# Key-feature sums from a Gram product, and six more split products of w_out, in an attention and SwiGLU kernel

## The chip, the core and the metric

The kernel is one program for one core of a Trainium2 chip. The metric is the device time of one execution in microseconds (us); three runs of the kernel before gave 276.74, 276.76 and 276.82, so its time is the median, 276.76. All profile rows are from one profiled execution of that kernel.

Engines are named as the profile names them: PE (TensorE, matmuls), PEld (its weight loads), DVE (VectorE), ACT (ScalarE), POOL (GpSimd), SP (SyncE, which issues DMAs). Every engine works through its own queue in order.

## What is computed

Four batches of four heads, 1088 positions, 32 numbers each, go through a linear attention, and its output through a SwiGLU block.

```python
def phi(x):                                   # 64 features from two sketches of 8
    a = np.einsum('rd,bhsd->bhsr', S1, x)
    b = np.einsum('rd,bhsd->bhsr', S2, x)
    return np.einsum('bhsi,bhsj->bhsij', a, b).reshape(*x.shape[:-1], r * r)
q_p, k_p = phi(q), phi(k)
kv = np.einsum('bhsf,bhsd->bhfd', k_p, v)
z = np.sum(k_p, axis=2)                       # the feature sums
num = np.einsum('bhsf,bhfd->bhsd', q_p, kv)
den = np.einsum('bhsf,bhf->bhs', q_p, z)[..., None] + 1e-06
x = (num / den)  ->  (4352, 128)
g = x @ w_gate                                # 128 -> 1536
out = (g * sigmoid(g) * (x @ w_val)) @ w_out  # 1536 -> 128
```

`z` for features i, j of one head is the sum over positions of `a_i * b_j`, which is an entry of the 8 x 8 matrix product of `a` transposed and `b`.

## The kernel before, in words

Everything is written out by hand in one order; nothing is scheduled afterwards. The 4352 tokens are cut into ten blocks: three small ones of batch 1 (384, 320, 384 tokens), then six of 480 and a last one of 384. The 1536 hidden features are twelve chunks of 128. One block and one chunk make a **unit**: two products (gate and value) of the block's x with 128 columns of the weights, a Silu on ACT, a product on DVE (the hidden chunk, into a slot of `hbuf`), and later a **down** product of the hidden chunk with 128 rows of `w_out` into a PSUM bank that collects the block's output.

The units of the last seven blocks are the loop at L1405 and are numbered y = 0 to 83 here: block `line[m]`, chunk j is y = 12 m + j. Each step of that loop starts unit y + 1 (`start_unit`, L983), finishes unit y (`finish_unit`, L994) and does one down product, that of unit y - 5.

**Split products.** A float32 product costs two instructions of two passes each. For the weights and for x the kernel uses three float32r products instead: a number is cut into a high part, a low part and a difference, and the exact product is put together from `wd*xd`, `w1*x1` and `wb*x0`. In a unit these are the two products of L989, a scaling by ACT in place in PSUM (L992), then four products (L1001, L1002); then Silu (L1004, ACT) and the hidden product (L1009, DVE), which frees the unit's pair of PSUM banks. Three such pairs go round, so unit y + 3 starts in the pair of unit y.

The down product is either plain (L1077, float32) or split (L1069, L1071, L1072), as the list `DOWN` says (L888 to L890): 6 chunks of `line[2]`, 9 each of `line[3]` to `line[5]`, 7 of the last block. For a split one, `cut_hidden` (L951) cuts the hidden chunk three steps ahead: h1 by ACT (L968) or DVE (L966) at step y + 1, h0 by POOL (L969) at y + 2, hd by DVE (L972) at y + 3. The parts lie in six sets of three tiles, taken in turn, in buffers that were used for loading k, q, v and for early hidden chunks. `w_out` is cut by `cut_down` (L903) in steps y = 20 to 28, into a tile that takes the place of `room`. In a block with split products the plain ones use `scaled`, a copy of `w_out` times -1, because the block is put together by a subtraction (L1105).

**Attention of batches 2 to 4** runs beside the units, in a generator (`attentions`, L615) that is stepped once per unit, from y = 20 on once in two. For a batch: transposes of k on DVE (L327), key sketches on PE (L354), copied out by ACT (L590; L630 for batch 2, which copies one of the two sketches and leaves the other in PSUM), the 64 features per key on DVE (L377), their products with v (`key_values`, L388), and the feature sums: POOL adds nine pieces (L547), four products with ones add the partitions (L713), and `fold` (L597) multiplies by the first sketch matrix and adds over i with three DVE instructions, into a column block of `s123`. `query_sketches` (L342) then gives numerator sketches and denominator at once. `query_step` (L737) makes the query features on DVE (L741 to L748, then L377 and the transposes of L758 in three pieces), and `numerators` (L766) multiplies them (L776) and copies x out. `numerators` stands at y = 4, 20 and 40. x itself is cut by ACT (L865), POOL (L868) and DVE (L873).

Of the kernel before, what the change touches and what calls it, by code (L numbers as in the profile page):

```python
# [7 lines left out]
FP32 = mybir.dt.float32  # L8
# [11 lines left out]
def kernel(  # L20
# [129 lines left out]
    wg = const.tile([P, NCH, P], FP32, name="wg")  # L150
    wv = const.tile([P, NCH, P], FP32, name="wv")
# [159 lines left out]
    NL = 10  # L311
    hbuf = const.tile([P, NH - NL, BW], FP32, name="hbuf")
    late = const.tile([P, NL, BW], FP32, tag="late", name="late", bufs=1)
    slots = [(hbuf[:, k, :] if k < NH - NL else late[:, k - NH + NL, :]) for k in range(NH)]
# [8 lines left out]
    own2 = const.tile([P, 2 * H], FP32, name="own2")  # L323
# [219 lines left out]
    def feature_sums(phk):  # L543

        rows = phk[:].rearrange("p c h i j -> p c (h i j)")
        s = apool.tile([P, 4, H * F], FP32, tag="zs", name="zs")[:, 0:2, :]
        add = lambda o, a, b: nc.gpsimd.tensor_tensor(out=o, in0=a, in1=b, op=ALU.add)  # L547

        def last():
            add(s[:, 0, :], s[:, 0, :], s[:, 1, :])  # L550
            add(s[:, 0, :], s[:, 0, :], rows[:, 8, :])

        return s[:, 0, :], [
            lambda: add(s, rows[:, 0:2, :], rows[:, 2:4, :]),
            lambda: add(s, s, rows[:, 4:6, :]),
            lambda: add(s, s, rows[:, 6:8, :]),
            last,
        ]

    def beside(gen, steps):  # L560

        for x in gen:
            if steps:
                steps.pop(0)()
            yield x

# [30 lines left out]
    def fold(kv):  # L597

        t = apool.tile([P, R, R], FP32, tag="fold", name="fold")
        w = apool.tile([P, R], FP32, tag="w", name="w")  # L600
        nc.vector.tensor_tensor(
            out=t[:], in0=kv[:, F : 2 * F].rearrange("p (i j) -> p i j", j=R),
            in1=sq[:, 0, :, :], op=ALU.mult,
        )
        nc.vector.tensor_reduce(
            out=w[:], in_=t[:].rearrange("p i j -> p j i"), axis=AX.X, op=ALU.add
        )
        nc.vector.tensor_tensor(
            out=s123[:, :, 2, :],
            in0=w[:].unsqueeze(1).to_broadcast([P, 2 * H, R]),  # L610
            in1=own2[:].unsqueeze(2).to_broadcast([P, 2 * H, R]),
            op=ALU.mult,
        )

    def attentions():  # L615
# [5 lines left out]
        for i, c in enumerate(kpieces):  # L621
            key_products(kp[:, i, :], *c)
        ka = apool.tile([P, NC * H, R], FP32, tag="kas", name="kas")

        def sketch(ps, i):
            c0, c1 = kpieces[i]
            return ps[:, i, 0 : 64 * (c1 - c0)].rearrange("p (x t r) -> p x t r", t=2, r=R)

        for i, (c0, c1) in enumerate(kpieces):
            nc.scalar.copy(ka[:, H * c0 : H * c1, :], sketch(kp, i)[:, :, 0, :])  # L630
        yield from turn_queries(1)
        phk = apool.tile([P, NC, H, R, R], FP32, tag="phk", name="phk")
        for n, (i, c0, c1) in enumerate(((0, 0, 3), (0, 3, 5), (1, 5, 7), (1, 7, 9))):
            first = H * (c0 - kpieces[i][0])
            kb = sketch(kp, i)[:, first : first + H * (c1 - c0), 1, :]
            key_features(phk, (ka[:, H * c0 : H * c1, :], kb), c0, c1)
            if n == 0:
                zs, sums = feature_sums(phk)
            else:
                sums.pop(0)()  # L640
            if n == 3:
                let_go("keys")
            if n % 3 != 1:
                yield
        sums.pop(0)()
        yield from turn_keys(2)
        kvz = pair("values")
        key_values(kvz[:, 0, 0:F], phk, 0, NC)
        kab, copies = sketched(pair(), key_products, 2, "kab2")
        run_copies(copies, 2)  # L650
        value_sums(kvz[:, 0, :], zs)
        fold(kvz[:, 0, :])
# [12 lines left out]
        zs, sums = feature_sums(phk)  # L665
        for f in sums:
            f()
        yield from turn_keys(3)
        yield from turn_queries(2)
        for b in (2, 3):  # L670
            yield "pe"
            if b == 3:
                numerators(2, spread)
            kv = bank("g2")
            key_values(kv[:, 0:F], phk, 0, NC)
            if b == 2:
                kab, copies = sketched(pair(), key_products, 2, "kab2")
                run_copies(copies, 2)
            value_sums(kv, zs)
            fold(kv)  # L680
            spread = spread_out(b, kv)
            yield
            yield "pe"
            qab, copies = sketched(pair(), query_sketches, 3, "qab")
            run_copies(copies, 2)
            yield
            if b == 2:
                yield from turn_queries(3)
# [20 lines left out]

    def value_sums(kv, zs):  # L710

        for h in range(H):
            nc.tensor.matmul(  # L713
                kv[32 * h : 32 * h + 32, F : 2 * F], ones[:], zs[:, F * h : F * h + F],
                start=True, stop=True,
            )
# [186 lines left out]
    def cut_down():  # L903

        n = len(FINE)
        parts = const.tile([P, 3, n, D], F32R, tag="room", name="dparts", bufs=1)
        w1, wb, wd = (parts[:, k] for k in range(3))
        scaled = apool.tile([P, len(PLAIN), D], FP32, tag="zs", name="scaled")
        low = const.tile([P, n, D], FP32, tag="late", name="dlow", bufs=1)
        down_parts.update(w1=w1, wb=wb, wd=wd, scaled=scaled)  # L910
        rest = [(0, slice(0, 1)), (1, slice(1, 8, 2)), (5, slice(6, 7)), (6, slice(NCH - 1, NCH))]

        def high(c):
            nc.scalar.activation(w1[:, c], wo[:, FINE[0] :][:, c], AF.Copy, scale=CUT)

        def left(c):
            nc.gpsimd.tensor_tensor(
                out=low[:, c], in0=wo[:, FINE[0] :][:, c], in1=whole(w1[:, c]), op=ALU.subtract
            )

        def scale(c):
            nc.scalar.activation(wb[:, c], low[:, c], AF.Copy, scale=BETA)

        def differ(c):
            nc.gpsimd.tensor_tensor(
                out=wd[:, c], in0=whole(w1[:, c]), in1=whole(wb[:, c]), op=ALU.subtract
            )

        def other(k, c):
            m = len(range(NCH)[c])  # L930
            nc.scalar.activation(scaled[:, k : k + m, :], wo[:, c, :], AF.Copy, scale=-1.0)


        def exchange():
            for k, c in zip((1, 3, 4), (8, 9, 10)):
                PLAIN[k] = c
                nc.scalar.activation(scaled[:, k, :], wo[:, c, :], AF.Copy, scale=-1.0)

        add_to(behind, NCH * 5 + 8, exchange)

        a, b, c = slice(0, 3), slice(3, 6), slice(6, n)
        for step in (
            [(high, a)], [(left, a), (high, b)], [(left, b), (scale, a)], [(differ, a), (high, c)],
            [(left, c), (scale, b)], [(differ, b), (scale, c)], [(differ, c), (other, *rest[0])],
            [(other, *rest[1])], [(other, *rest[2]), (other, *rest[3])],
        ):
            for f, *args in step:
                f(*args)
            yield

    def cut_hidden(y, i, j):  # L951

        if not h_sets:
            x = []
            for tag in ("kld", "qld", "vld", "kT", "qT"):
                t = const.tile([P, 2, WB], F32R, tag=tag, name="h" + tag, bufs=1)
                x += [t[:, k, :] for k in range(2)]
            t = const.tile([P, 8, WB], F32R, tag="late", name="hlate", bufs=1)
            x += [t[:, k, :] for k in range(8)]
            h_sets.extend(x[k : k + 3] for k in range(0, 18, 3))  # L960
# [4 lines left out]
        if j in (2, 5, 8, 10) and i != line[2]:  # L965
# [11 lines left out]
    room = const.tile([P, 10, BW], FP32, tag="room", name="room", bufs=1)  # L977
# [39 lines left out]
    def unit(i, j, late=False, between=(None, None), apart=False):  # L1017
# [10 lines left out]
        sg = room[:, len(lates) + caught[0], :] if late else fpool.tile([P, WB], FP32, tag="sg", name="sg", bufs=5)  # L1028
# [25 lines left out]
    def down(y=None):  # L1054
# [11 lines left out]
        if j in mine:  # L1066
            w1, wb, wd = [down_parts[x][:, FINE.index(j), :] for x in ("w1", "wb", "wd")]
# [7 lines left out]
        else:  # L1075
            w = down_parts["scaled"][:, PLAIN.index(j), :] if mine else wo[:, j, :]
# [390 lines left out]
```

## Time and profile before

| What | Value |
|---|---|
| time, median of 3 runs | 276.76 us (276.74 to 276.82) |
| the profiled execution, span from first to last instruction | 275.1 us |
| PE, DVE, ACT, POOL busy | 268.8, 214.1, 193.6, 105.7 us |
| granted TensorE clock | 1.00 in every stretch, 0.97 in the last 9 us |

The profile gives no device time of the profiled execution apart from its span, so 1.66 us of the median lie around the span.

Busy time of the engines by stretch of the span (us):

| Stretch | what runs | PE | DVE | ACT | POOL |
|---|---|---|---|---|---|
| 48 to 70 | last units of the first blocks, keys of batch 2 | 22.00 of 22 | 20.28 | 10.46 | 12.30 |
| 70 to 108 | into the loop, batch 2 queries, keys of batch 3 | 38.00 of 38 | 27.59 | 25.76 | 12.06 |
| 108 to 143 | y = 8 to 21 | 35.00 of 35 | 24.77 | 22.59 | 7.28 |
| 143 to 183 | y = 21 to 39, `cut_down`, batch 4 queries | 39.92 of 40 | 28.86 | 34.35 | 17.55 |
| 183 to 266 | y = 40 to 83 | 83.00 of 83 | 71.86 | 70.78 | 40.77 |

How to read it. A busy PE is not a PE at its peak, since matmuls are pipelined. What one product costs the kernel is the time from its start to the start of the next one, which the chain of work that ended last gives, instruction by instruction. A row of a timeline has start, duration, engine, line, operation and shape; two rows of one engine may overlap a little, so that a product of 0.65 us on DVE takes 0.57 us of its queue. In brackets stands what idle time before it waited for.

### The profile page before, as it was taken

The numbers are of one execution on the slowest core, as the hardware profiler recorded it, in microseconds if no ns is written. First come the engines' busy times: TensorE is split into PE (matmuls) and PEld (weight loads), VectorE is DVE, ScalarE is ACT, GpSimd is POOL, SyncE is SP. The second block draws the span as 40 slices with busy tenths as digits, with TensorE's granted clock in tenths as the row PEclk, the third lists the DMA queues.
The fourth block names the chain that finished last, engine by engine and source line by source line (L and its number), as shares of the span: only waits on it lengthen the run. The fifth ranks groups of instructions, "written<-read, shape, count | busy, mean of one in ns | idle before, by whom it ended". The sixth has DMA issues, their size and how long they took to land.

```text
span 275.1 us, 5788 instructions
## 1 busy us (share of the span) xinstructions
PE 268.8 (98%) x2191; PEld 200.5 (73%) x2191; DVE 214.1 (78%) x373; ACT 193.6 (70%) x349; POOL 105.7 (38%) x117
## 2 busy tenths in 40 slices
PE   7999999999999999999999999999999999999995
PEld 6645566666785786777577777867887888789994
DVE  3997988989788773887545766967987995998871
ACT  2468666462685686677479898769879888897880
POOL 3313422149350640260034353435535663553330
PEclk9999999999999999999999999999999999999999
DMA  6573196122231043000200020000100200010021
GB/s 191 172 216 87 49 270 200 60 104 62 62 88 23 4 111 99 2 0 0 38 12 4 1 38 0 0 2 11 26 2 0 36 1 0 13 25 1 2 36 29
DMA packets 26139, 14.30 MB, mean 52 GB/s; under 512 B 19840, under 2 KB 24192, under 8 KB 26112
## 3 DMA queue, kind: packets, MB, share of 16 engines
q1 hardware_dynamic: 25456, 13.84, 19.6%
q8 instruction: 17, 0.28, 0.4%
q10 hardware_dynamic: 656, 0.10, 0.2%
q14 instruction: 10, 0.08, 0.1%
HBM read 11.41 MB, written 2.23 MB: 50 GB/s over the span
## 4 chain that ended last, share of the span: by engine, by line
PE 93%; DVE 3%; DMA 2%; ACT 1%; issue 0%; SPq 0%
PE PS L1077 20%; PE PS L1001 14%; PE PS L989 14%; PE PS L1002 14%; PE PS L1025 12%; PE PS L1072 3%; PE PS L1071 3%; PE PS L1069 3%; PE PS L354 2%; PE PS L776 2%; PE PS L342 2%; DMA kld<-in_k_dram 2%; PE PS L388 2%; PE PS L1117 1%; PE PS L497 1%; PE PS L445 1%
## 5 line engine op out<-in xcount | busy, mean ns | idle before, releaser
L992 ACT ACTIVATE PS<-PS 128x960 f32<-128x960 f32 (+1 forms) x90 | 83.3, 926 | 29.8 <-PE PS L989 28.8
L1009 DVE SCALAR_TENSOR_TENSOR hbuf<-PS,sg 128x480 f32<-128x480 f32 (+1 forms) x87 | 55.2, 634 | 36.6 <-ACT sg L1004 36.1
L1004 ACT ACTIVATE sg<-PS 128x480 f32<-128x480 f32 (+1 forms) x90 | 49.6, 551 | 1.6 <-PE PS L1002 1.2
L1077 PE MATMUL PS<-hbuf,wo 128*128 128x480 f32 (+2 forms) x94 | 39.4, 516 | 0.0
L989 PE MATMUL PS<-xd,graw 128*128 128x480 f32 (+1 forms) x69 | 37.5, 543 | 0.0
L989 PE MATMUL PS<-xd,wd 128*128 128x480 f32 (+1 forms) x90 | 33.6, 373 | 0.0
L1002 PE MATMUL PS<-x,wb 128*128 128x480 f32 (+1 forms) x90 | 33.5, 372 | 0.0
L1001 PE MATMUL PS<-x,w 128*128 128x480 f32 (+1 forms) x90 | 33.4, 371 | 0.0
L1002 PE MATMUL PS<-x,graw 128*128 128x480 f32 (+1 forms) x69 | 25.5, 370 | 0.0
L989 PEld LDWEIGHTS PS<-xd,wd 128*128 128x128 f32 x90 | 17.0, 189 | 9.9 <-issue 5.3
L1025 PE MATMUL PS<-xT,wg 128*128 128x384 f32 (+1 forms) x60 | 23.5, 473 | 0.1
L1025 PE MATMUL PS<-xT,wv 128*128 128x384 f32 (+1 forms) x60 | 23.2, 467 | 0.3 <-DVE wv L286 0.3
L868 POOL TENSOR_TENSOR x<-xT,x 128x480 fp32r<-128x480 f32 (+1 forms) x6 | 7.2, 1195 | 37.8 <-ACT x L865 37.8
L1077 PEld LDWEIGHTS PS<-hbuf,wo 128*128 128x128 f32 x94 | 17.7, 189 | 5.4 <-issue 0.4
L1029 ACT ACTIVATE sg<-PS 128x384 f32<-128x384 f32 (+1 forms) x24 | 11.2, 468 | 13.2 <-PE PS L1025 12.4
L969 POOL TENSOR_TENSOR hlate<-hbuf,hlate 128x480 fp32r<-128x480 f32 (+1 forms) x12 | 14.6, 1218 | 11.0 <-ACT hlate L968 9.7
L989 PEld LDWEIGHTS PS<-xd,graw 128*128 128x128 f32 x69 | 13.0, 188 | 7.6 <-ACT PS L992 4.1
L1001 PEld LDWEIGHTS PS<-x,w 128*128 128x128 f32 x90 | 16.9, 187 | 2.2
L1002 PEld LDWEIGHTS PS<-x,wb 128*128 128x128 f32 x90 | 16.9, 188 | 2.1
L1001 PE MATMUL PS<-x,graw 128*128 128x480 f32 (+1 forms) x48 | 18.1, 376 | 0.0
L1077 PE MATMUL PS<-hbuf,scaled 128*128 128x480 f32 (+1 forms) x40 | 17.1, 518 | 0.0
L1025 PEld LDWEIGHTS PS<-xT,wv 128*128 128x128 f32 x60 | 11.2, 190 | 7.4 <-DVE hbuf L1040 0.8
(205 smaller groups left out, 572.0 us busy)
## 6 DMA issues: line engine op xcount, KB each, us to landing
kld<-in_k_dram SPq DMA_DIRECT2D x4, 544.0 KB, 4.4
vld<-in_v_dram SPq DMA_DIRECT2D x12, 144.0 KB, 4.3
qld<-in_q_dram SPq DMA_DIRECT2D x3, 544.0 KB, 4.8
raw<-in_moe_w_out_dram SPq DMA_DIRECT2D x4, 384.0 KB, 4.4
raw<-in_moe_w_gate_dram SPq DMA_DIRECT2D x3, 384.0 KB, 3.3
raw<-in_moe_w_val_dram SPq DMA_DIRECT2D x3, 384.0 KB, 3.5
out_dram<-o SPq DMA_DIRECT2D x16, 60.0 KB, 2.0
vld<-in_v_dram SPq DMA_DIRECT2D x4, 112.0 KB, 4.1
```

Of the source, the lines that this page charges most:

```text
L969: add_to(before, y + 2, lambda: nc.gpsimd.tensor_tensor(out=h0, in0=h, in1=whole(h1), op=ALU.subtract))
L989: nc.tensor.matmul(ps[:, k], w_parts[id(w), j // 3][2][:, j % 3, :], xd, start=True, stop=True)
L992: nc.scalar.activation(ps, ps, AF.Copy, scale=-1.0 / WHOLE)
L1001: nc.tensor.matmul(ps[:, k], w1, x1, start=False, stop=False, skip_group_check=True)
L1002: nc.tensor.matmul(ps[:, k], wb, x0, start=False, stop=True, skip_group_check=True)
L1004: nc.scalar.activation(sg, ps[:, 0], AF.Silu, scale=WHOLE)
L1009: nc.vector.scalar_tensor_tensor(out=hj[:, 0:n], in0=ps[:, 1], scalar=WHOLE, in1=sg, op0=ALU.mult, op1=ALU.mult)
L1025: nc.tensor.matmul(o[:, 0:n], w[:, j, :], xT[:, t0 : t0 + n], start=True, stop=True)
L1029: nc.scalar.activation(sg[:, 0:n], g[:, 0:n], AF.Silu)
L1069: nc.tensor.matmul(acc[i][:, 0:n], wd, hd, **sides)
L1071: nc.tensor.matmul(p, w1, h1, start=(j == mine[0]), stop=False)
L1077: nc.tensor.matmul(acc[i][:, 0:n], w, hidden[i, j][:, 0:n], **sides)
```

## The change

Four edits.

1. The feature sums of batches 2 to 4 no longer come from POOL. `gram` multiplies the first sketches of four heads with the second sketches, nine products of 32 x 32 that are spread over four column groups of PE and start before `key_values`; ACT copies the result (32 columns); `fold` multiplies it with a turned, repeated copy of the first sketch matrix on PE and masks it by one DVE product. `turn_sketch` makes that copy once, just ahead of batch 2's key products: ACT writes a repeated copy, PE turns it, ACT copies it out. Batch 2 takes both sketches out of PSUM with ACT, as the other batches do.
2. `w_out` is cut into parts with the sign turned (`wb - w1`), so that the block is put together by an addition and the plain products use `wo` itself; `scaled` and its copies go. The cutting is in five groups at y = 9, 13, 16, 20 and 23, four steps each, into the buffers of `wv` and `wg` (no longer read then) and one tile of its own.
3. The parts of hidden chunks lie in seven sets (five until `line[2]`), which are added one by one. The tile `late` is divided into `late` and `feats`, `room` into `room` and `low`, so that buffers come free one at a time.
4. `DOWN` has 46 chunks in place of 40: 8, 9 and 10 of `line[1]` (y = 20 to 22) and 1, 5 and 7 of `line[2]` (y = 25, 29, 31). In these two blocks h1 is made by ACT, for j = 9 by DVE.

The order of the instructions of PE is otherwise the same, and so is that of SP.

```diff
-    def feature_sums(phk):
-        rows = phk[:].rearrange("p c h i j -> p c (h i j)")
-        s = apool.tile([P, 4, H * F], FP32, tag="zs", name="zs")[:, 0:2, :]
-        add = lambda o, a, b: nc.gpsimd.tensor_tensor(out=o, in0=a, in1=b, op=ALU.add)
...
+    def turn_sketch(ps):
+        four = apool.tile([P, 4, H, R], FP32, tag="fold", name="four")
+        nc.scalar.copy(four[:], s12[:, :, 0, :].unsqueeze(1).to_broadcast([P, 4, H, R]))
+        nc.tensor.matmul(
+            ps, four[:].rearrange("p a h r -> p (a h r)"), ident[:], start=True, stop=True
+        )
+        nc.scalar.copy(sketch_turned[:], ps)
+
+    def gram(kv, kab):
+        flat = "p x r -> p (x r)"
+        for c in range(NC):
+            x, a = slice(H * c, H * c + H), c % 4
+            nc.tensor.matmul(
+                kv[32 * a : 32 * a + 32, F : F + H * R],
+                kab[:, 0, x, :].rearrange(flat), kab[:, 1, x, :].rearrange(flat),
+                start=(c < 4), stop=(c >= NC - 4),
+            )
+        g = apool.tile([P, H * R], FP32, tag="gram", name="gram")
+        nc.scalar.copy(g[:], kv[:, F : F + H * R])
+        return g
+
+    def fold(kv, g):
+        ps = kv[:, 2 * F : 2 * F + H * R]
+        nc.tensor.matmul(ps, sketch_turned[:], g[:], start=True, stop=True)
         nc.vector.tensor_tensor(
+            out=s123[:, :, 2, :].rearrange("p (x h) r -> p x h r", x=2),
+            in0=ps.rearrange("p (x h r) -> p x h r", x=1, r=R).to_broadcast([P, 2, H, R]),
+            in1=own[:].unsqueeze(1).unsqueeze(3).to_broadcast([P, 2, H, R]),
             op=ALU.mult,
         )
...
         yield from turn_keys(1)
         kp = pair("keys")
+        turn_sketch(kp[:, 1, 320 : 320 + P])
+        kab, copies = sketched(kp, key_products, 2, "kab2")
+        run_copies(copies, 2)
...
             kv = bank("g2")
+            g = gram(kv, kab)
             key_values(kv[:, 0:F], phk, 0, NC)
...
-            value_sums(kv, zs)
-            fold(kv)
+            fold(kv, g)
...
-    DOWN = [(line[2], j) for j in (2, 4, 6, 8, 9, 10)]
-    DOWN += [(i, j) for i in line[3:6] for j in (1, 2, 4, 5, 6, 7, 8, 9, 10)]
+    DOWN = [(line[1], j) for j in (8, 9, 10)]
+    DOWN += [(i, j) for i in line[2:6] for j in (1, 2, 4, 5, 6, 7, 8, 9, 10)]
     DOWN += [(LAST, j) for j in range(1, 8)]
...
+    def cut_down(c0, c1, home, low):
+        n = c1 - c0
+        w1, wb, wd = (home[:, n * k : n * k + n, :] for k in range(3))
...
+        nc.scalar.activation(w1, src, AF.Copy, scale=CUT)
+        yield
+        nc.gpsimd.tensor_tensor(out=low, in0=src, in1=whole(w1), op=ALU.subtract)
+        yield
+        nc.scalar.activation(wb, low, AF.Copy, scale=BETA)
+        yield
+        nc.gpsimd.tensor_tensor(out=wd, in0=whole(wb), in1=whole(w1), op=ALU.subtract)
...
+        if len(h_sets) < (5 if i < line[2] else OWN):
+            h_sets.insert(0, next(h_rooms))
...
-        if j in (2, 5, 8, 10) and i != line[2]:
+        if j in ((2, 5, 8, 10) if i > line[2] else (9,)):
             add_to(before, y + 1, lambda: nc.vector.tensor_scalar(h1, h, CUT, None, op0=ALU.mult))
...
-        join = lambda: nc.vector.scalar_tensor_tensor(
-            out=x, in0=d, scalar=-1.0, in1=x, op0=ALU.mult, op1=ALU.add
-        )
+        join = lambda: nc.vector.tensor_tensor(out=x, in0=d, in1=x, op=ALU.add)
...
+    for y0, c0, c1, where in (
+        (9, 8, 11, ("wv", 0)), (13, 4, 5, ("wg", 9)), (16, 1, 2, ("wv", 9)), (20, 2, 4, ("rest", 0)),
+        (23, 5, 8, ("wg", 0)),
+    ):
+        for k in range(4):
+            down_steps.setdefault(y0 + k, []).append((k, c0, c1, *where))
```

More of the change, by code (lines that the diff above doesn't have):

```diff
@@ L149 @@
     sraw = const.tile([2 * R, Dh], S1.dtype, name="sraw")
-    wg = const.tile([P, NCH, P], FP32, name="wg")
-    wv = const.tile([P, NCH, P], FP32, name="wv")
+    wg = const.tile([P, NCH, P], FP32, tag="wg", name="wg", bufs=1)
+    wv = const.tile([P, NCH, P], FP32, tag="wv", name="wv", bufs=1)
     wo = const.tile([P, NCH, D], FP32, name="wo")
@@ L310 @@
     NH = 27
-    NL = 10
+    NL, NF = 10, 6
     hbuf = const.tile([P, NH - NL, BW], FP32, name="hbuf")
-    late = const.tile([P, NL, BW], FP32, tag="late", name="late", bufs=1)
-    slots = [(hbuf[:, k, :] if k < NH - NL else late[:, k - NH + NL, :]) for k in range(NH)]
+    late = const.tile([P, NL - NF, BW], FP32, tag="late", name="late", bufs=1)
+    feats = const.tile([P, NF, BW], FP32, tag="feats", name="feats", bufs=1)
+    slots = [x[:, k, :] for x, n in ((hbuf, NH - NL), (late, NL - NF), (feats, NF)) for k in range(n)]
     slot_of = {}
@@ L322 @@
     s123 = const.tile([P, 2 * H, 3, R], FP32, name="s123")
-    own2 = const.tile([P, 2 * H], FP32, name="own2")
     sq = const.tile([P, 2, R, R], FP32, name="sq")
@@ L541, in divide @@
             part(name, 0)
-    def feature_sums(phk):
-        rows = phk[:].rearrange("p c h i j -> p c (h i j)")
-        s = apool.tile([P, 4, H * F], FP32, tag="zs", name="zs")[:, 0:2, :]
-        add = lambda o, a, b: nc.gpsimd.tensor_tensor(out=o, in0=a, in1=b, op=ALU.add)
[L549 to L565, printed above, removed]
     def turn_keys(b):
@@ L595, in sketched @@
         return t, [(copy, i, *c) for i, c in enumerate(kpieces)]
-    def fold(kv):
-        t = apool.tile([P, R, R], FP32, tag="fold", name="fold")
-        w = apool.tile([P, R], FP32, tag="w", name="w")
-        nc.vector.tensor_tensor(
-            out=t[:], in0=kv[:, F : 2 * F].rearrange("p (i j) -> p i j", j=R),
-            in1=sq[:, 0, :, :], op=ALU.mult,
-        )
[L605 to L611, printed above, removed]
+    sketch_turned = const.tile([P, P], FP32, name="s1t")
+    def turn_sketch(ps):
[20 more added lines that the diff above has]
+        nc.tensor.matmul(ps, sketch_turned[:], g[:], start=True, stop=True)
+        nc.vector.tensor_tensor(
+            out=s123[:, :, 2, :].rearrange("p (x h) r -> p x h r", x=2),
+            in0=ps.rearrange("p (x h r) -> p x h r", x=1, r=R).to_broadcast([P, 2, H, R]),
+            in1=own[:].unsqueeze(1).unsqueeze(3).to_broadcast([P, 2, H, R]),
             op=ALU.mult,
@@ L620, in attentions @@
         kp = pair("keys")
[L621 to L630, printed above, removed]
+        turn_sketch(kp[:, 1, 320 : 320 + P])
+        kab, copies = sketched(kp, key_products, 2, "kab2")
+        run_copies(copies, 2)
+        let_go("keys")
         yield from turn_queries(1)
         phk = apool.tile([P, NC, H, R, R], FP32, tag="phk", name="phk")
[L633 to L645, printed above, removed]
+        yield from features(phk, kab)
         yield from turn_keys(2)
         kvz = pair("values")
+        g = gram(kvz[:, 0, :], kab)
         key_values(kvz[:, 0, 0:F], phk, 0, NC)
@@ L650, in attentions @@
         run_copies(copies, 2)
-        value_sums(kvz[:, 0, :], zs)
-        fold(kvz[:, 0, :])
+        fold(kvz[:, 0, :], g)
         spread = spread_out(1, kvz[:, 0, :])
@@ L664, in attentions @@
         yield from features(phk, kab)
-        zs, sums = feature_sums(phk)
-        for f in sums:
-            f()
         yield from turn_keys(3)
@@ L688, in attentions @@
                 yield from turn_queries(3)
-                phk = late[:, NL - 6 :, :].rearrange("p s (n h i j) -> p (s n) h i j", h=1, i=R, j=R)
+                phk = feats[:].rearrange("p s (n h i j) -> p (s n) h i j", h=1, i=R, j=R)
                 phk = phk.rearrange("p (c h) o i j -> p c (h o) i j", h=H)
                 yield from features(phk, kab)
-                zs, sums = feature_sums(phk)
-            yield from beside(query_step(b, qab), sums)
+            yield from query_step(b, qab)
         yield "pe"
@@ L708, in features @@
                 yield
[L710 to L716, printed above, removed]
     def spread_out(b, kv):
@@ L886 @@
     line = list(range(HEAD, len(blocks)))
-    FINE, PLAIN = range(1, NCH - 1), [0, 1, 3, 5, 7, 6, NCH - 1]
-    DOWN = [(line[2], j) for j in (2, 4, 6, 8, 9, 10)]
-    DOWN += [(i, j) for i in line[3:6] for j in (1, 2, 4, 5, 6, 7, 8, 9, 10)]
+    DOWN = [(line[1], j) for j in (8, 9, 10)]
+    DOWN += [(i, j) for i in line[2:6] for j in (1, 2, 4, 5, 6, 7, 8, 9, 10)]
     DOWN += [(LAST, j) for j in range(1, 8)]
@@ L901, in now @@
             f()
[L903 to L949, printed above, removed]
@@ L951, in cut_hidden @@
-    def cut_hidden(y, i, j):
[L953 to L960, printed above, removed]
+    def cut_down(c0, c1, home, low):
+        n = c1 - c0
+        w1, wb, wd = (home[:, n * k : n * k + n, :] for k in range(3))
+        for k in range(n):
+            down_parts[c0 + k] = [x[:, k, :] for x in (w1, wb, wd)]
+        src = wo[:, c0:c1, :]
+        nc.scalar.activation(w1, src, AF.Copy, scale=CUT)
[5 more added lines that the diff above has]
+        nc.gpsimd.tensor_tensor(out=wd, in0=whole(wb), in1=whole(w1), op=ALU.subtract)
@@ new lines, in more_room, with ground @@
+    def more_room():
+        def ground(tag, n):
+            t = const.tile([P, n, WB], F32R, tag=tag, name="h" + tag, bufs=1)
+            return [t[:, k, :] for k in range(n)]
+        x = ground("room", 6)
+        yield x[:3]
+        yield x[3:]
+        yield ground("late", 3)
+        x = ground("kld", 2) + ground("kT", 2)
+        yield x[:3]
+        x = x[3:] + ground("qld", 2)
+        yield x
+        x = ground("vld", 2) + ground("qT", 2)
+        yield x[:3]
+        yield ground("feats", 4)[:3]
@@ L961, in cut_hidden @@
+    h_rooms = more_room()
+    OWN = 7
+    def cut_hidden(y, i, j):
+        if len(h_sets) < (5 if i < line[2] else OWN):
+            h_sets.insert(0, next(h_rooms))
         n = SPLIT if i == LAST else blocks[i][1]
@@ L974, in cut_hidden @@
         ))
-    room = const.tile([P, 10, BW], FP32, tag="room", name="room", bufs=1)
+    rooms = [
+        const.tile([P, n, BW], FP32, tag=tag, name=tag, bufs=1) for tag, n in (("room", 8), ("low", 2))
+    ]
+    room = [x[:, k, :] for x, n in zip(rooms, (8, 2)) for k in range(n)]
     sums_of = {}
@@ L1027, in unit @@
             )
-        sg = room[:, len(lates) + caught[0], :] if late else fpool.tile([P, WB], FP32, tag="sg", name="sg", bufs=5)
+        sg = room[len(lates) + caught[0]] if late else fpool.tile([P, WB], FP32, tag="sg", name="sg", bufs=5)
         nc.scalar.activation(sg[:, 0:n], g[:, 0:n], AF.Silu)
@@ L1066, in down @@
         if j in mine:
-            w1, wb, wd = [down_parts[x][:, FINE.index(j), :] for x in ("w1", "wb", "wd")]
+            w1, wb, wd = down_parts[j]
             h1, h0, hd = h_parts.pop((i, j))
@@ L1075, in down @@
         else:
-            w = down_parts["scaled"][:, PLAIN.index(j), :] if mine else wo[:, j, :]
-            nc.tensor.matmul(acc[i][:, 0:n], w, hidden[i, j][:, 0:n], **sides)
+            nc.tensor.matmul(acc[i][:, 0:n], wo[:, j, :], hidden[i, j][:, 0:n], **sides)
         if i != LAST:
@@ L1104, in put_together @@
         acc[i] = x
-        join = lambda: nc.vector.scalar_tensor_tensor(
-            out=x, in0=d, scalar=-1.0, in1=x, op0=ALU.mult, op1=ALU.add
-        )
+        join = lambda: nc.vector.tensor_tensor(out=x, in0=d, in1=x, op=ALU.add)
         if i == LAST:
@@ L1208 @@
         nc.gpsimd.tensor_copy(s123[:, h : h + H, 0:2, :], s12[:])
-        nc.gpsimd.tensor_copy(own2[:, h : h + H], own[:])
     for c in (c0, c1):
@@ L1294, in free @@
     def free(c):
-        return [room[:, c, :].rearrange("p (c f) -> p c f", f=P)]
+        return [room[c].rearrange("p (c f) -> p c f", f=P)]
     w = ("wg", "wv")
@@ L1403, with settle @@
             token_steps.setdefault(at, []).append(gen)
-    down_steps = cut_down()
+    home = {}
+    def settle(tag, n=NCH):
+        if tag not in home:
+            home[tag] = const.tile([P, n, D], FP32 if tag == "low" else F32R, tag=tag, name="d" + tag, bufs=1)
+        return home[tag]
+    down_steps = {}
+    for y0, c0, c1, where in (
[4 more added lines that the diff above has]
+            down_steps.setdefault(y0 + k, []).append((k, c0, c1, *where))
+    cutting = {}
     for y in range(END):
@@ L1421 @@
             next(gen, None)
-        if y in range(20, 30):
-            next(down_steps, None)
+        for k, c0, c1, tag, t0 in down_steps.get(y, ()):
+            if k == 0:
+                n = c1 - c0
+                parts_at = settle(tag, NCH if tag != "rest" else 6)[:, t0 : t0 + 3 * n, :]
+                low_at = settle("low", 6)[:, 3 * (c0 >= 8) :, :][:, 0:n, :]
+                cutting[c0] = cut_down(c0, c1, parts_at, low_at)
+            next(cutting[c0], None)
     ps = wide("a")[:, 0, 0:D]
```

## The prediction

> **What bounds the kernel now.** I read the busy times first, then the shares of the chain of work that ended last.
>
> ```profile
> PE 268.8 (98%) x2191; PEld 200.5 (73%) x2191; DVE 214.1 (78%) x373; ACT 193.6 (70%) x349; POOL 105.7 (38%) x117
> ...
> PE 93%; DVE 3%; DMA 2%; ACT 1%; issue 0%; SPq 0%
> ```
>
> PE sets the end. After the first slices it has no gap, so an edit is worth the PE time that it saves or costs, plus any gap that it opens. DVE, ACT and POOL cost nothing until PE waits for them. The chain in order of time prices a product, as the time until the next one starts (start, us, what):
>
> ```profile
> 188.14 0.81 PE PS L1077 x2
> 188.95 0.43 PE PS L989 x2
> ...
> 190.26 0.21 PE PS L1069
> 190.47 0.21 PE PS L1071
> 190.69 0.22 PE PS L1072
> 190.91 0.43 PE PS L989 x2
> ```
>
> A plain down costs 0.81 us, a split one 0.21 + 0.21 + 0.22 = 0.65 (190.26 to 190.91). Around batch 2 the chain shows the key products (L354), the key-value products (L388) and the four products with ones (L713):
>
> ```profile
> 52.63 0.65 PE PS L1077 x2
> 53.28 1.20 PE PS L354 x36
> ...
> 66.61 1.14 PE PS L388 x72
> 67.76 1.20 PE PS L354 x36
> 68.95 0.25 PE PS L713 x8
> ```
>
> **PE's own terms.** Order on PE and SP is unchanged but for these, and no DMA is added or moved.
>
> - Six more split downs: 6 x (0.65 - 0.81) = -0.93.
> - L713 goes: 0.25, 0.25 and, for batch 4, 0.11 and some 0.12 of the next product (0.41 at 138.63, where its like takes 0.22, because tiles go back to full size) = -0.73.
> - `gram`, three times 18 instructions. The nearest row is L388: 72 in 1.14, 15.9 ns each, with 64 columns. A gram product has 32; the price lies between half of the row and all of it, 0.14 to 0.29. I take 0.17, near the half, as the columns are: +0.50 (0.42 to 0.86).
> - The product in `fold`, three times. The nearest is a 128-column float32 product at 0.11 per instruction (L1117), here with 32 columns: 0.05 to 0.22 for its two, I take 0.14, +0.42 (0.15 to 0.66). For batch 4 the return from small tiles to full ones, hidden in L713's price until now, adds some 0.1 again.
> - `turn_sketch` stands before L354 at 53.28. Its product has 2 x 0.11 = 0.22. PE also waits for ACT's copy, which no row of before shows. ACT works here until 53.4:
>
> ```profile
> 52.41 0.61 ACT L268 ACTIVATE exp<-exp,rebias 128x384 int32<-128x384 int32 x1
> 52.92 0.51 ACT L269 ACTIVATE man<-man 128x384 f32<-128x384 int32 x1
> ```
>
> The nearest copy of 128 x 128 by ACT (L931) takes 0.31, so the copy ends at 53.7 and PE waits some 0.4. Term: +0.65; 0.22 if the copy is earlier in ACT's queue, 0.8 if it is later. Behind the waiting product stand the key products, and all of PE.
>
> Sum: -0.93 - 0.73 + 0.50 + 0.42 + 0.1 + 0.65 = 0.0. All low ends together give -0.87 (the return to full tiles at nothing too), all high ends +0.76.
>
> **What leaves and joins the other engines.** POOL loses the piece sums (L547), some 18 us between 62 and 122, which no product of PE waits for while it has its cover; DVE loses two of three instructions of each `fold`; ACT loses `scaled`. ACT gains three copies of the Gram product (32 columns each; the L630 row at 54.52 takes 0.27 for 128, I estimate 0.22). In batches 2 and 3 L388 and L354, 1.14 + 1.20 us, hide the copy. In batch 4 only L388 hides it (72 instructions, 1.03 after the gram), with ACT busy with L793 until 138.12: copy at 138.35, PE ready at about 138.5. Without that cover it costs up to 0.3. Batch 2's larger copies, 0.4 in place of 0.29, lie in ACT idle time (0.63 and 0.17 before the two L630 rows). The cutting of `w_out` goes from y = 20 to 28 to y = 9 to 26: 20 operations, of which most fall in 108 to 143, where ACT has 22.6 of 35 us busy and POOL 7.3, of which the sums leave. I cost it at nothing.
>
> **The gap that I expect.** Each split down brings DVE one hd (L972), POOL one h0 (L969, 1.22 us) and ACT or DVE one h1. These are no PE time, but the hidden product (L1009) of unit y frees the PSUM pair in which unit y + 3 starts, and it stands behind hd in DVE's queue. Between the end of y's four products and the start of y + 3 lie 0.65 + 0.43 + 0.87 + 0.65 = 2.6 us in split steps; L1009 takes 0.57 of the queue, so it may start up to 2.0 after the products' end. Usually it starts 1.0 after (193.25, products' end 192.22), late in batch 4's queries 1.6 (175.08 against 173.5): no gap in before, but 0.4 from it.
>
> DVE's and POOL's timelines at 207 to 213 show why hd is dearer than it looks:
>
> ```profile
> 203.87 0.64 DVE L972 SCALAR_TENSOR_TENSOR hqT<-hkT,hbuf 128x480 fp32r<-128x480 f32 x1
> ...
> 209.62 1.04 DVE L873 SCALAR_TENSOR_TENSOR xd<-x,xT 128x480 fp32r<-128x480 f32 x1
> 210.58 1.68 DVE L972 SCALAR_TENSOR_TENSOR hlate<-hqT,hbuf 128x480 fp32r<-128x480 f32 x1
> ```
>
> ```profile
> 207.74 1.22 POOL L868 TENSOR_TENSOR x<-xT,x 128x480 fp32r<-128x480 f32 x1 [4.87 <-ACT x L865]
> 208.92 1.23 POOL L969 TENSOR_TENSOR hlate<-hbuf,hqT 128x480 fp32r<-128x480 f32 x1
> 210.09 1.64 POOL L969 TENSOR_TENSOR hlate<-hbuf,hlate 128x480 fp32r<-128x480 f32 x1
> ```
>
> The same hd takes 0.64 with POOL idle and 1.68 when POOL works: xd, begun at 209.62, ends 0.51 after POOL's row does (210.15); POOL's next one, begun at 210.09, takes 1.64 since xd is in its way; and hd, begun at 210.58, ends 0.53 after that one (211.73). Two operations that both read two operands from SBUF go one after the other, on DVE and POOL; L1009, with one operand in PSUM, always takes 0.65. The key and query features (L377) are of the first kind: 2.00 at 172.59, beside an h0 at 172.56. In 190 to 206, seven h0 lengthened DVE's work by about 4.4 us in all, 0.63 each, and DVE was 15.16 of 16 busy; PE had no gap, for nothing else was on DVE.
>
> The Trainium skill, page "SBUF — State Buffer", section "Who interferes with whom", states that GpSimd and VectorE share one pair of ports as an exclusive lock, held for a whole instruction, so that the other blocks entirely. The rows above agree (0.64 against 1.68). By the rule each of the six new h0 could hold DVE for its whole length, 7.3 us, against 3.8 at the rows' mean; it speaks against this change.
>
> In the changed kernel y = 30 to 36 are all split, so h0 comes in every step, and the query work of batch 4 stands in the same steps: L377 after y = 30 and 34, the transposes (L758, 0.95) after 28, 32 and 36, xd of the next block (L873) near y = 32, h1 by DVE at y = 33. From L1009 of y = 30 to that of y = 35 DVE has five L1009 (2.85), five hd (2.85), two L377 (1.75), one transpose (0.9), xd (0.55) and h1 (0.35): 9.3 us, against 5 x 1.95 = 9.8 of PE. Before, the steps of y = 30 and 31 did not all have parts (1, 5 and 7 were plain), and POOL rested between h0s. With waits of 0.63 for each of five h0, 3.15, DVE falls 9.3 + 3.15 - 9.8 = 2.65 behind, of which 1.0 is slack (2.0 allowed, 1.0 used): a gap of about 1.6. If every h0 goes ahead of DVE's operation, for its whole 1.22 in three steps and some 0.77 in the two where DVE is also on a transpose or h1, the waits are 5.2 and the gap 3.7; if none does, no gap. I take the steady stretch's mean, as the row with the same operations: **+1.6**. It shows as gaps before L989 in units 33 to 38 and is not given back, since PE has no idle time later. Later blocks are as before.
>
> **Forecast.** 275.1 + 1.66 around the span = 276.76, the median; 276.76 + 0.0 + 1.6 = 278.4 us, slower.
>
> **Rivals.**
>
> - *Even.* DVE's queue absorbs the waits, because L1009 is in time: gap below 0.3, PE's terms near 0. For it: before, seven h0 in 190 to 206 stall nothing. Against it: there, no query work. 276.8. Chance 0.22 (same 0.14, faster 0.05, slower 0.03).
> - *Faster.* The same without a gap, and PE's small products at their low ends: gram 0.42, fold 0.15, `turn_sketch` 0.22 because ACT gets to its copy before L268. That is -0.87 and 275.9. For it: 32 columns are half of L388's; against it: ACT's rows at 52.41 and 52.92 stand just ahead of the copy. It decides if PE shows no gap at 53.3 and none in y = 33 to 38. Chance 0.20.
> - *Not what it says.* The Gram product's copy comes after PE needs it (batch 4), or split downs in y = 20 to 31 still start late for their parts, and the -0.93 isn't had: 276.76 + 0.93 = 277.7. Chance 0.03.
> - Forecast's case: chance 0.55; with all waits against DVE 276.76 + 3.7 = 280.5.
>
> **How the numbers follow.** Low end: the faster rival, 275.9. High end: the forecast's case with all waits, 280.5. What lies outside, beyond both, I put at 0.2. A measurement here can tell some 0.2% (0.55 us) from no change. Faster by more: 0.20 + 0.05 = 0.25. Within: 0.14. Slower: 0.55 + 0.03 + 0.03 = 0.61.
>
> **What would show it.** The changed profile should have split rows (0.65) in the downs of y = 20 to 22, 25, 29 and 31; a gap of 0.4 and a 0.22 product ahead of L354 near 53.3; gram in 0.14 to 0.29 and fold in 0.05 to 0.22; PE gaps before L989 in units 33 to 38, ended by DVE's hidden product, with hd and L377 rows of 1.3 to 2.0 beside h0 there. I am wrong if PE has no gap there, or if a gap stands elsewhere: before down products that wait for hd, or before numerators.

## The result, and the profile after

The changed kernel takes 283.7 us (median of 5 runs, 283.42 to 283.95) against 276.82 in the runs beside it: ratio 1.024, interval 1.0224 to 1.0257. The forecast was 278.4 with a range of 275.9 to 280.5: the sign was right, the size (+1.6) was a quarter of the +6.9 measured, and the time lies above the range.

The page of the changed kernel, busy times and the shares of the chain:

```profile
PE 270.2 (96%) x2235; PEld 202.6 (72%) x2235; DVE 221.1 (79%) x376; ACT 195.7 (69%) x356; POOL 98.7 (35%) x110
...
PE 83%; DVE 9%; ACT 3%; issue 2%; DMA 1%; SPq 0%; DVEq 0%; ACTq 0%
```

PE has 1.4 us more work, but its share of the chain fell from 93% to 83%: PE now waits. The waits of PE say for whom (line, releaser: us in total, times, longest):

```profile
PE PS L388 <- ACT gram L595: 2.8, 3, 1.3
PE PS L937 <- DVE hbuf L957: 1.8, 2, 1.1
...
PE PS L1024 <- POOL wo L286: 0.5, 1, 0.5
...
PE PS L579 <- ACT four L578: 0.4, 1, 0.4
```

None of these four rows is in the profile of before. L937 (start_unit) behind the hidden product and L579 (`turn_sketch`) behind ACT were forecast. The largest, `key_values` (L388) behind ACT's copy of the Gram product, was not, nor was the down product (L1024) behind POOL's last piece of `w_out`. The chain through batch 2 shows the first:

```profile
67.23 0.53 ACT graw L812
67.76 0.50 DVE graw L815
68.26 0.48 DVE low L810
68.74 0.02 issue
68.76 0.52 ACT graw L812
69.28 0.09 ACT gram L595
69.37 0.04 issue
69.41 1.21 PE PS L388 x72
70.62 1.20 PE PS L354 x36
71.82 0.34 PE PS L601 x2
```

L388 starts as soon as ACT's copy ends, and the copy stood in ACT's queue behind the cutting of gate weights (L812), which waited for DVE. In batch 3 a cut of x (0.60) stood there, in batch 4 the two copies of L757 (0.70). The forecast read this cover the wrong way round: it let L388 hide the copy.

To place the +6.9, I compare the starts of like instructions in the two traces. From 52 us on the changed kernel loses 6.95 (in its profiled run the first 52 us were 0.38 shorter, because the first key products started at 5.96 in place of 6.34; the traces of this case have 5.89 to 6.41 there):

| Term | forecast | measured | where |
|---|---|---|---|
| six split downs | -0.93 | about -0.9 | 0.145 each, from e6 below |
| `gram`, three times, with what it makes wait | +0.50 | +3.65 | 67.83 to 69.41, 100.67 to 101.88, 141.48 to 142.34 |
| L713 away, `fold` product in | -0.2 | +0.3 | 0.34 each for L601 |
| `turn_sketch` | +0.65 | +0.88 | down to key products 1.62, before 0.74 |
| key features of batch 2 | 0 | +0.72 | L354 to the next products 14.05, before 13.33 |
| gaps behind the hidden product | +1.6 | +2.4 | units of y = 36 and 38 |
| sum | +1.6 | +7.0 | |

### The profile page after: what moved, and what is told of

The parts are those of the page before. It is cut to its first block, busy times and chain, and to the rows that moved or that the text cites. A ratio compares the mean times of both kernels' runs of the same rounds, so it can differ in the third digit from the quotient of the medians.

```text
span 281.7 us, 5882 instructions
## 1 busy us (share of the span) xinstructions
PE 270.2 (96%) x2235; PEld 202.6 (72%) x2235; DVE 221.1 (79%) x376; ACT 195.7 (69%) x356; POOL 98.7 (35%) x110
## 4 chain that ended last, share of the span: by engine, by line
PE 83%; DVE 9%; ACT 3%; issue 2%; DMA 1%; SPq 0%; DVEq 0%; ACTq 0%
PE PS L1024 15%; PE PS L937 13%; PE PS L949 13%; PE PS L950 13%; PE PS L973 10%; PE PS L1017 3%; PE PS L1019 3%; PE PS L1020 3%; PE PS L354 2%; PE PS L740 2%; PE PS L342 2%; PE PS L388 2%; DMA kld<-in_k_dram 1%; DVE phk L377 1%; DVE hbuf L957 1%
## 5 line engine op out<-in xcount | busy, mean ns | idle before, releaser
L1024 PE MATMUL PS<-hbuf,wo 128*128 128x480 f32 (+3 forms) x122 | 50.7, 512 | 0.0
L937 PE MATMUL PS<-xd,graw 128*128 128x480 f32 (+1 forms) x69 | 36.0, 521 | 0.0
L937 PE MATMUL PS<-xd,wd 128*128 128x480 f32 (+1 forms) x90 | 34.0, 377 | 1.8 <-DVE hbuf L957 1.8
L1024 PEld LDWEIGHTS PS<-hbuf,wo 128*128 128x128 f32 x122 | 22.8, 189 | 5.9 <-issue 0.4
L937 PEld LDWEIGHTS PS<-xd,wd 128*128 128x128 f32 x90 | 17.0, 188 | 11.3 <-issue 4.5
L914 POOL TENSOR_TENSOR hroom<-hbuf,hroom 128x480 fp32r<-128x480 f32 (+1 forms) x14 | 17.2, 1229 | 8.8 <-ACT hroom L913 4.3
L937 PEld LDWEIGHTS PS<-xd,graw 128*128 128x128 f32 x69 | 13.0, 188 | 6.8 <-ACT PS L940 3.2
L973 PEld LDWEIGHTS PS<-xT,wg 128*128 128x128 f32 x60 | 10.9, 190 | 7.8 <-issue 1.1
```

The source lines that it names most:

```text
L914: add_to(before, y + 2, lambda: nc.gpsimd.tensor_tensor(out=h0, in0=h, in1=whole(h1), op=ALU.subtract))
L937: nc.tensor.matmul(ps[:, k], w_parts[id(w), j // 3][2][:, j % 3, :], xd, start=True, stop=True)
L973: nc.tensor.matmul(o[:, 0:n], w[:, j, :], xT[:, t0 : t0 + n], start=True, stop=True)
L1024: nc.tensor.matmul(acc[i][:, 0:n], wo[:, j, :], hidden[i, j][:, 0:n], **sides)
```

## The experiments

Theory after the result: four separate losses, of which the wait of `key_values` for the Gram copy is the largest; the gaps behind the hidden product come, as forecast, from DVE and POOL that hold each other up. Rivals stand with each run. In all, the time of before beside the runs was 276.86 to 276.97.

**e1, gram behind key_values.**

```diff
-            g = gram(kv, kab)
             key_values(kv[:, 0:F], phk, 0, NC)
+            g = gram(kv, kab)
```

> The changed kernel with gram issued behind key_values in place of ahead of it, in all three batches. Theory: the changed kernel is slower mostly because key_values waits until ACT has copied the Gram product out of the PSUM bank into which key_values writes (gaps of 1.27 + 0.91 + 0.57 = 2.75 us before L388). Behind key_values the copy lies beside the next batch's key products (1.20 us) in batches 2 and 3, and only fold of batch 4 still waits, some 0.3 to 0.5. So 283.7 - 2.75 + 0.4 = 281.3 us (281.0 to 281.7), with no wait before L388. Rival: the copy is late because ACT's queue is full there, and the wait goes to fold instead, in the same size: 283.4 to 284.

Measured: 281.64 us (281.0 to 282.45), ratio 1.0155 (1.0113 to 1.0196). Batch 2's chain in e1:

```profile
68.16 1.14 PE PS L388 x72
69.30 0.17 PE PS L589 x18
69.47 1.20 PE PS L354 x36
70.67 0.34 PE PS L601 x2
```

No wait is left before L388, and `fold` (L601) follows the key products without one: the order made the wait. Only in batch 4, with no key products between, `fold` waits 0.29. Here `gram` costs 0.17, as forecast. The times of e1 spread over 1.45 us, and its profiled run has one pause in L342 with no releaser (0.30 idle, 0.55 lost), which no other trace shows.

**e2, another bank.**

```diff
-        g = gram(kvz[:, 0, :], kab)
+        g = gram(kvz[:, 1, :], kab)
```

> The changed kernel with the Gram product of batch 2 alone in the other PSUM bank of the pair that key_values uses; order unchanged. If the wait goes with the bank, the gap of 1.27 us before batch 2's L388 goes, while fold has the copy ready: 283.7 - 1.27 = 282.4 us (282.2 to 282.7). If it goes with the tile (the pair is one), or if something else than the copy holds key_values back, the gap stays and so does the time: 283.4 to 284.

Measured: 282.25 us (282.07 to 282.44), ratio 1.0173 (1.0131 to 1.0215). The wait row and the chain of e2:

```profile
PE PS L388 <- ACT gram L595: 1.5, 2, 0.9
```

```profile
68.19 0.31 PE PS L589 x18
68.50 1.08 PE PS L388 x72
69.58 1.20 PE PS L354 x36
70.78 0.34 PE PS L601 x2
```

Three waits became two; batch 2's is gone though order, tile and ACT's queue are as they were. So the wait belongs to the PSUM bank: ACT reads columns 64 to 95 of it, `key_values` writes 0 to 63. The Trainium skill, page "PSUM — Partial Sum Buffer", section "PSUM bank collisions raise a hardware error", says that PSUM has to be guarded by bank and quarter of the partitions, not by address. That is the rule that the forecast lacked, and e2 agrees with it: 1.27 us by bank alone. What the two would do without the wait was not tried.

**e3, no low parts in line[2].**

```diff
+        if i == line[2]:
+            h_parts[i, j][1] = h1
+        else:
             add_to(before, y + 2, lambda: nc.gpsimd.tensor_tensor(
```

> The changed kernel without POOL's low parts (h0) of the block line[2], y = 24 to 35; its split products take h1 in place of h0, so PE, DVE and ACT have all their instructions, and the block's values are wrong by the low part. Theory: the gaps of 0.76 and 1.08 us before start_unit around y = 34 and 37 come from h0 on POOL and hd, L377 on DVE holding each other up; without h0 both go, hd takes 0.65 throughout, and with the slower restarts 2.1 us are gained: 281.6 us (281.4 to 281.9). Rival: DVE has too much work there even without waits, gaps of over 1 us stay: 282.6 to 283.7.

Measured: 281.14 us (281.06 to 281.22), ratio 1.0135 (1.01 to 1.017): 2.56 less than the changed kernel, a little more than expected. Both gaps are gone. POOL's and DVE's timelines in the changed kernel, then DVE's in e3 at the same units:

```profile
175.10 1.27 POOL L914 TENSOR_TENSOR hlate<-hbuf,hlate 128x480 fp32r<-128x480 f32 x1 [0.72 <-ACT hlate L913]
178.49 1.24 POOL L914 TENSOR_TENSOR hkld<-hbuf,hkld 128x480 fp32r<-128x480 f32 x1 [2.12 <-PE PS L950]
180.04 1.59 POOL L914 TENSOR_TENSOR hqld<-hbuf,hkT 128x480 fp32r<-128x480 f32 x1 [0.31 <-ACT hkT L913]
```

```profile
173.78 0.96 DVE L722 STREAM_TRANSPOSE phT<-phq 128x768 f32<-128x768 f32 x1
174.67 0.61 DVE L837 SCALAR_TENSOR_TENSOR xd<-x,xT 128x480 fp32r<-128x480 f32 x1
175.21 1.69 DVE L917 SCALAR_TENSOR_TENSOR hroom<-hroom,hbuf 128x480 fp32r<-128x480 f32 x1
176.81 0.65 DVE L957 SCALAR_TENSOR_TENSOR hbuf<-PS,sg 128x480 f32<-128x480 f32 x1
...
178.83 1.71 DVE L377 TENSOR_TENSOR phq<-qab 128x768 f32<-128x768 f32 x1
180.47 1.68 DVE L917 SCALAR_TENSOR_TENSOR hlate<-hlate,hbuf 128x480 fp32r<-128x480 f32 x1
182.07 0.65 DVE L957 SCALAR_TENSOR_TENSOR hbuf<-PS,sg 128x480 f32<-128x480 f32 x1
```

```profile
174.62 0.65 DVE L920 SCALAR_TENSOR_TENSOR hroom<-hroom,hbuf 128x480 fp32r<-128x480 f32 x1
175.19 0.65 DVE L960 SCALAR_TENSOR_TENSOR hbuf<-PS,sg 128x480 f32<-128x480 f32 x1
...
177.31 0.95 DVE L377 TENSOR_TENSOR phq<-qab 128x768 f32<-128x768 f32 x1
178.17 0.65 DVE L920 SCALAR_TENSOR_TENSOR hlate<-hlate,hbuf 128x480 fp32r<-128x480 f32 x1
178.74 0.65 DVE L960 SCALAR_TENSOR_TENSOR hbuf<-PS,sg 128x480 f32<-128x480 f32 x1
```

DVE has the same operations in both. In the changed kernel an h0 on POOL (L914) stands beside each of the three long ones; without h0 hd takes 0.65 in place of 1.68, L377 0.95 in place of 1.71, and DVE even waits for ACT again (0.63 before 180.59). DVE does not have too much work; it is held up.

**e4, feature sums as before.** The diff is the reverse of edit 1, with `zs` in the two pieces that it uses and batch 2's copied sketch in the tile of `kab2`.

```diff
-            g = gram(kv, kab)
             key_values(kv[:, 0:F], phk, 0, NC)
...
-            fold(kv, g)
+            value_sums(kv, zs)
+            fold(kv)
```

> The changed kernel with the feature sums as before (POOL adds the pieces, four products with ones, fold on DVE, batch 2's second sketch read from PSUM); the 46 split products, their buffers and the earlier cutting of w_out stay. Theory: this leaves the six split products (-0.65 measured in the changed kernel between y = 20 and 32) and the gaps of y = 34 to 38 (+2.08): 276.8 - 0.65 + 2.08 = 278.2 us (277.9 to 278.6). Rival: the moved cutting of w_out or the buffers cost something of their own, or POOL's sums take longer beside them: 279 or more. A second rival: the gaps came from POOL's new free time, and go: 276.1.

Measured: 278.19 us (277.95 to 279.67), ratio 1.004 (1.0021 to 1.0058). In its trace units run within 0.06 us of before's from 73 to 148 us, so the other buffers, the earlier cutting and POOL's sums beside it cost nothing; at y = 32 it is 0.53 ahead (the first four new split downs), and after the unit of y = 38 1.5 behind. So 283.7 - 278.19 = 5.5 us are the Gram product, and the rest is the gaps less the split downs. With POOL's sums back the gaps are 0.68 and 1.10 (0.76 and 1.08 in the changed kernel), so POOL's free time had no part in them.

**e5, e6, e7, e10: fewer split products**, on e4. The chunks of `line[2]` left out are 7 (e5), 5 and 7 (e6), 1, 5 and 7 (e7), 5 (e10). The edit of e6:

```diff
+    LESS = [(line[2], 5), (line[2], 7)]
...
-    DOWN += [(i, j) for i in line[2:6] for j in (1, 2, 4, 5, 6, 7, 8, 9, 10)]
+    DOWN += [(i, j) for i in line[2:6] for j in (1, 2, 4, 5, 6, 7, 8, 9, 10) if (i, j) not in LESS]
```

> e4 without the split product of chunk 7 of line[2] (y = 31), so 45 of them and one pair of h0 on POOL and hd on DVE less between y = 33 and 34. Theory: DVE's queue falls behind step by step because h0 comes in every step; one pause ahead of y = 33's hidden product gives back about 1.2 us of queue, so the first gap (0.68, before the unit of y = 36) goes and the second (1.10) shrinks: the splits' -0.5 and a gap of 0 to 0.6, that is 276.97 - 0.5 + 0.3 = 276.8 us (276.4 to 277.1). Rival: both gaps are due to L377 and h0 of their own step alone, and stay: 278.2.

> e4 without chunks 5 and 7 of line[2] (y = 29 and 31): 44 split products, a pause of POOL in two steps. Theory: no gap of the first kind and none or up to 0.5 of the second: 276.97 - 0.4 + 0.2 = 276.8 us (276.4 to 277.0). If the gaps depend only on the steps y = 33 to 35, the result is that of e5 plus 0.1.

> e4 with the six chunks of line[2] that the kernel before has, so 43 split products, three new ones of line[1]. Theory: no gaps, as in the kernel before, since line[2] is as there; three split products at -0.10 to -0.155 each: 276.97 - 0.4 = 276.6 us (276.4 to 276.8). Rival: the earlier cutting of w_out and the other buffers open gaps or hold back split products: 277 or more.

> e4 without chunk 5 of line[2] (y = 29) alone: 45 split products with chunk 7 (y = 31) kept. e5, without chunk 7, kept a first gap of 0.68 and half of the second; e6, without both, has none. Theory: chunk 5 decides, since its hd and h0 meet batch 4's second L377 and make DVE late ahead of the transpose and xd; without it no gap of over 0.3: 276.08 - 0.1 = 276.0 us (275.8 to 276.3). Rival: each of the two chunks brings about half of the gaps, and one alone leaves 0.7 to 1.2: 276.8 to 277.4.

| Run | split downs | us (lowest to highest) | ratio to before | gaps behind the hidden product |
|---|---|---|---|---|
| e4 | 46 | 278.19 (277.95 to 279.67) | 1.004 (1.0021 to 1.0058) | 0.68, 1.10 |
| e5, without 7 | 45 | 277.66 (277.35 to 278.47) | 1.0022 (1.0003 to 1.0042) | 0.68, 0.52 |
| e10, without 5 | 45 | 277.05 (276.76 to 278.92) | 1.0004 (0.9984 to 1.0025) | none, 0.77 |
| e6, without 5 and 7 | 44 | 276.08 (275.87 to 276.88) | 0.9973 (0.9957 to 0.9988) | none |
| e7, without 1, 5, 7 | 43 | 276.3 (276.08 to 277.9) | 0.999 (0.9973 to 1.0008) | none |

My expectations of e5 and e10 both fell: neither chunk alone is the cause. e6 and e7 came out below the ranges expected of them, which both began at 276.4. Chunk 5 brings the whole first gap; of the second, 0.77 is there without chunk 5 and 0.52 without chunk 7. The trace of e5 says why the pause that I had counted on came too late: chunk 7's h0 would stand on POOL between 167 and 169, but DVE is already late by L377 (1.84 at 163.72) and chunk 5's hd (1.09 at 166.62), which the h0 of chunks 5 and 6 (163.52 and 165.49 on POOL) stretch. In e6 the same L377 has no h0 beside it:

```profile
163.85 0.93 DVE L378 TENSOR_TENSOR phq<-qab 128x768 f32<-128x768 f32 x1
164.71 0.64 DVE L955 SCALAR_TENSOR_TENSOR hqT<-hvld,hbuf 128x480 fp32r<-128x480 f32 x1
165.27 0.65 DVE L995 SCALAR_TENSOR_TENSOR hbuf<-PS,sg 128x480 f32<-128x480 f32 x1
167.04 0.66 DVE L995 SCALAR_TENSOR_TENSOR hbuf<-PS,sg 128x480 f32<-128x480 f32 x1 [1.12 <-ACT sg L990]
```

e6, expected at 276.8 because of a rest of the second gap, has none, and is the one version here that is measurably faster than both kernels. Its four new split downs gain 0.58 in the trace (0.32 to 0.90 ahead of before between y = 19 and 38), 0.145 each, where the forecast had 0.155.

**e8, batch 2's second sketch from PSUM**, on e1. Gram's copy of it stays.

```diff
-        let_go("keys")
...
-        yield from features(phk, kab)
+        for n, (i, c0, c1) in enumerate(((0, 0, 3), (0, 3, 5), (1, 5, 7), (1, 7, 9))):
...
+            kb = ps[:, H * (c0 - k0) : H * (c1 - k0), 1, :]
+            key_features(phk, (kab[:, 0, H * c0 : H * c1, :], kb), c0, c1)
...
```

> e1 (gram behind key_values) with batch 2's key features reading the second sketch from PSUM, as in the kernel before, beside the copy that gram needs. Theory: with both sketches in SBUF the features (L377) and POOL's operations hold each other up between 58 and 66 us (L377 2.08 for two of 512 columns in place of 1.27, POOL's two L810 2.99 in place of 1.96), so the last piece of w_out is ready late and PE waits 0.45 before L1024 near 63.6. From PSUM this goes: 281.64 - 0.45 = 281.2 us (281.0 to 281.4), L377 back to 1.3. Rival: the wait for w_out comes from ACT's or DVE's other shifts there (turn_sketch), and stays: 281.6.

Measured: 280.0 us (279.67 to 281.21), ratio 1.012 (1.0091 to 1.0148), 1.0 below the range that I expected. DVE's L377, first in the changed kernel, then in e8:

```profile
62.43 2.08 DVE L377 TENSOR_TENSOR phk<-kab 128x512 f32<-128x512 f32 x2
```

```profile
62.26 1.27 DVE L377 TENSOR_TENSOR phk<-kab,PS 128x512 f32<-128x512 f32 x2
```

The wait for `w_out` is gone, and batch 2's products stand where they stood before (13.34 us behind L354; e1 14.06). The edit is worth 0.72 by the traces, more than the 0.45 of the wait row. The 1.3 between the two profiled spans (279.6 and 278.3) holds e1's pause of 0.55 too; the medians differ by 1.64, but e1's times spread too widely for that to be the price. The second operand's place, PSUM or SBUF, decided whether DVE met POOL.

**e9, the Gram product eased**: e8 with 44 split downs, as e6, and with ACT's repeated copy for `turn_sketch` ahead of the transposes.

```diff
+        four = apool.tile([P, 4, H, R], FP32, tag="fold", name="four")
+        nc.scalar.copy(four[:], s12[:, :, 0, :].unsqueeze(1).to_broadcast([P, 4, H, R]))
         yield from turn_keys(1)
         kp = pair("keys")
-        turn_sketch(kp[:, 1, 320 : 320 + P])
+        turn_sketch(kp[:, 1, 320 : 320 + P], four)
...
```

> e8 with 44 split products (without chunks 5 and 7 of line[2], as e6) and ACT's repeated copy for turn_sketch issued ahead of the transposes of batch 2's keys: the Gram product with all its avoidable waits taken away. Theory: 280.0 - 2.1 (e4 to e6) - 0.4 (wait of turn_sketch) = 277.5 us (277.1 to 277.8), still 1.4 above e6, because its own products cost PE more than the four products with ones: turn_sketch 0.49, gram 0.17 + 0.17 + 0.3 and a wait of 0.3 in batch 4, fold 3 x 0.34, together 2.4 against 0.73. Rival: the waits were the whole of it and the Gram product is as cheap as the sums: 276.1 to 276.4.

Measured: 277.24 us (276.97 to 278.72), ratio 1.0017 (1.0005 to 1.0029). The chain of e9 at `turn_sketch` (L577):

```profile
52.70 0.65 PE PS L1032 x2
53.35 0.22 PE PS L577 x2
53.57 1.20 PE PS L354 x36
```

0.22, not 0.88: the wait cost more than its gap of 0.39, since the product behind it then took 0.49. With these waits away (0.29 before batch 4's `fold` is left) the Gram product still costs 277.24 - 276.08 = 1.2 us more than the sums by POOL and four products with ones. The two profiled spans differ by 1.40, but 0.43 of that lies ahead of the first key products (6.41 against 5.98 us), long before the Gram product; behind them e9 loses 0.97. So its own cost is about 1.0 us.

## Why the prediction was wrong

- **Gram product: mechanism missed.** The step that failed is "In batches 2 and 3 L388 and L354, 1.14 + 1.20 us, hide the copy. In batch 4 only L388 hides it". L388 waits for the copy (wait row), because both use one PSUM bank (e2, in batch 2; with the other order of e1 the wait is gone in all three). The forecast gave this cover a bound, "without that cover it costs up to 0.3", for batch 4 alone. Its third rival has a copy that comes too late, but in batch 4 alone, and prices only the loss of the -0.93; no rival has `key_values` wait. Measured, `gram` with its wait costs 3.65 in place of 0.50. The product itself was sized rightly: 0.17 in e1, 0.31 in e2, ahead of L388.
- **`fold`: mis-sized.** 0.34 each in place of 0.14, so the exchange with L713 loses 0.3 rather than gaining 0.2. The chain row includes the change between a full-size product and small tiles, which the bounds by instruction left out.
- **`turn_sketch`: right, somewhat low.** Wait of 0.4 forecast, 0.39 measured; the products behind a wait took 0.49 in place of 0.22.
- **Batch 2's key features: missed.** I costed only the larger copies, at nothing, rightly; but the copy also moves an operand of L377 from PSUM to SBUF, and the same hold-up that I used for y = 30 to 36 then meets POOL's `w_out` work at 58 to 66: 0.72 (e8).
- **Gaps behind the hidden product: right mechanism, low.** Forecast as gaps of units 33 to 38, ended by DVE's hidden product; they came at the units of y = 36 and 38. Shown by e3. Size 2.4 against 1.6: between the steady stretch's mean and all waits (3.7). L377, counted as an operation of 0.87, is itself stretched by 0.89 and 0.76 (1.84 and 1.71 against 0.95 in e3). The mean of 0.63 also left out a row of its own stretch: h1 by DVE takes 0.87 at 190.01, beside the h0 of 189.37, and 0.40 at 197.00 with none beside it. With it the waits there are 4.9 us, 0.70 each, and the same sum gives a gap of 2.0. h1 reads one operand, so the prediction's rule of two operations with two operands from SBUF is too narrow.
- **Split downs: right.** 0.145 measured, 0.155 priced.
- **Buffers, cutting, POOL's freed time: right at nothing** (e4). All 18 us taken from POOL had been beside PE's work, and giving them back changed the two gaps by under 0.1.
- **The rivals.** The even and the faster rival both needed no gap in y = 33 to 38; both fell. The third had the split downs start late for their parts; they ran, and paid. The 0.2 left outside the range went to nothing named, and that is where the time was: with PE's terms at their high ends (+0.76) and all waits (3.7) the forecast's own sum reaches 281.2.

The Trainium skill's rule of the shared pair of ports, page "SBUF — State Buffer", section "Who interferes with whom", which the prediction cites, agrees with e3: beside h0s of 1.24 to 1.59 us the same hd and L377 lose 0.76 to 1.04 each.

## What to carry to other kernels

A copy out of PSUM that PE's next instructions do not read can still hold them, if they write the same bank: put it behind them, or in another bank, before counting them as its cover. Taking work off an engine that nobody waits for gains nothing, and what replaces it on the engine that sets the end is paid in full. When an operand moves from PSUM to SBUF, look again at every DVE operation that reads it beside POOL.

## What was not expected of the hardware

- A wait of PE costs more than its gap: `turn_sketch` lost 0.66 (0.88 against 0.22) for a gap of 0.39, and the two gaps of 0.76 and 1.08 some 2.4 together. The last product before a gap runs out (0.38 where 0.22 is its share of a full queue), and the first one behind it takes 0.49 in place of 0.38. PE's timeline around the first of the two:

```profile
176.37 0.38 PE L937 MATMUL PS<-xd,gphq 128*128 128x480 f32 x1
177.51 0.49 PE L937 MATMUL PS<-xd,wd 128*128 128x480 f32 x1 [0.76 <-DVE hbuf L957]
177.84 0.38 PE L949 MATMUL PS<-x,graw 128*128 128x480 f32 x1
```

- A pair of PSUM banks was freed by halves: in the changed kernel the gate product of a late unit (the half that ACT's Silu had read) had started (176.37 above), and only the value product waited for DVE. The chain shows one L937 of 0.49 behind each gap, where L937 x2 of 0.44 stands otherwise.
